# Attention beside a plain FFN: heads apart, and each weight piece converted over two steps

## The chip, the cores and the metric

The kernel runs on one core of one Trainium2 chip. The metric is the time of one execution on the device in microseconds, the median of the runs. The engines are called as the profile calls them: PE multiplies matrices (PEld loads its weights), DVE, ACT and POOL work on elements, and SP issues the transfers between HBM and the core's memory.

## The reference

Attention with a threshold over 8 batches and 8 heads (576 positions, head size 64), then one feed-forward layer with ELU over the 4608 tokens. The weights `w_in` (512 x 2048) and `w_out` (2048 x 512) arrive as 64-bit floats, everything else as 32-bit floats.

```python
scale = 1.0 / np.sqrt(q.shape[-1])
scores = scale * np.matmul(q, k.transpose(0, 1, 3, 2))
thresh = np.max(scores, axis=-1, keepdims=True) - tau
scores = np.where(scores >= thresh, scores, -1000000000.0)
scores = scores - np.max(scores, axis=-1, keepdims=True)
attn = np.exp(scores)
attn = attn / (np.sum(attn, axis=-1, keepdims=True) + 1e-09)
attn_out = np.matmul(attn, v)
x = attn_out.transpose(0, 2, 1, 3).reshape(B * S, H * D)
h = x @ w_in
g = np.where(h > 0.0, h, alpha * (np.exp(np.minimum(h, 0.0)) - 1.0))
out = g @ w_out
```

## The kernel before, in words

**Attention.** Two heads of a batch make a pair, and a pair is worked on in five *steps*: four of 128 query rows for both heads, and a fifth (i = 4) in which the last 64 rows of both heads fill one block of 128. In a step, PE makes the scores into PSUM (`scores`, tile `sc`); DVE takes each row's maximum (`mx`); from it come the bound of the mask (`th`, on POOL) and the bias of the exponential (`nb`); ACT makes the exponential `e`; DVE compares the scores with `th` and multiplies by `e` into `w`, with the row sum beside it (`masks`); DVE takes the reciprocal `rs`; POOL multiplies `w` by it (`normalize`). PE then turns `w` by blocks into the PSUM tiles `rt`, which ACT copies out (`turn_parts`, in two or three parts), and after two and five steps of a pair it multiplies by v (`values`, PSUM tile `pv`, copied out by ACT into `xt`). The tiles `pv` and `rt` share two PSUM buffers.

**Stages.** The first batch (20 steps) runs alone. The stage that the change touches is the next 15 steps, from `per_seq` to `SWITCH`; beside the attention of the second batch it runs the FFN of the first one in the plain way. Then come a stage of ten steps and the main stage, in which the FFN is done in another way with fewer products; the change leaves their work as it is, and only moves functions that the main stage defined to a place where both stages can use them.

**The FFN in this stage.** A unit of the first product (`ffn1`) is two halves of eight PE instructions each; when it is complete, ACT takes the exponential, POOL subtracts one (`minus`) and DVE makes the ELU by a minimum and a maximum (`elu`). A unit of the second product has two halves and no such work until its output is complete. `SHARES` says how many halves go into a step at each of three places: `after`, `second` and `carried`, whose work behind PE is left to the next step. `ffn_halves` takes a unit only when the weights that it needs are converted (`needs`). PE has two PSUM banks `f` for it.

**The weights.** A 64-bit float is loaded as two 32-bit words and made into a 32-bit float in pieces of 128 x 512, 32 in all. Each goes through a load into `wst` (four buffers, 512 KB), `convert_rest` (ACT, on the low words, in place), `convert_top` (DVE, two instructions into `wtop`, two buffers), `convert_add` (POOL), `convert_abs` (ACT, on the high words, in place) and `convert_end` (DVE, into the weight tiles). Six pieces are done in the first stage, and two in each step of this one. `load_w(4)` issues the next load if fewer than four pieces are loaded and not yet ended; the transfer has to wait until the piece that had the buffer before is ended.

**The order.** The stage is written under `manual_schedule`: each engine has one queue, and the instructions stand in it in the order in which the Python code emits them. In the kernel before, a step emits: loads of two pieces; scores; values; the first piece's top and add; the carried FFN work; the first turn; maxima of both heads in one instruction, `nb` and `th` on POOL, exponentials; the first piece's abs; FFN halves; the second piece's top, add and abs; the other turns and halves; masks; `minus`; both `convert_end`; `elu`; the normalize; the transposes and loads of the next pair (q in step i = 2, k in i = 3); and at last `convert_rest` of the two pieces of the next step. The scores of both heads lie in one PSUM tile of four banks, of which there is one.

Of the kernel before, what the change touches and what calls it, by code (L numbers as in the profile page):

```python
# [10 lines left out]
FP32 = mybir.dt.float32  # L11
U32 = mybir.dt.uint32
I32 = mybir.dt.int32
AF = mybir.ActivationFunctionType
# [5 lines left out]
def kernel(  # L20
# [90 lines left out]
    def load_w(ahead=2):  # L111
        i = progress[0]
        if i >= len(pieces) or i >= progress[1] + ahead:
            return
        progress[0] += 1
        src, dst, j, n = pieces[i]
        rows = src[j * P : (j + 1) * P]
        if src.dtype == FP32:
            nc.sync.dma_start(dst, rows[:, n : n + WN])
            return  # L120
        st = staged[i] = wstage.tile([P, WN, 2], U32, name="wst", bufs=4)
        nc.sync.dma_start(st.rearrange("p n w -> p (n w)"), rows.bitcast(U32)[:, 2 * n : 2 * (n + WN)])
# [8 lines left out]
    def convert_top(i):  # L131

        if i in staged:
            hi = staged[i][:, :, 1]
            top = tops[i] = wstage.tile([P, WN], U32, name="wtop", bufs=2)
            nc.vector.tensor_scalar(top, hi, 3, 0x3FFFFFFF, ALU.logical_shift_left, ALU.bitwise_and)
            nc.vector.scalar_tensor_tensor(top, hi, 0xC0000000, top, ALU.bitwise_and, ALU.bitwise_or)  # L137

    def convert_add(i):

        if i in staged:
            top = tops[i].bitcast(I32)
            nc.gpsimd.tensor_tensor(top, top, staged[i][:, :, 0].bitcast(I32), ALU.add)  # L143

    def convert_abs(i):
        if i in staged:
            mag = staged[i][:, :, 1].bitcast(FP32)
            nc.scalar.activation(mag, mag, AF.Abs)
# [95 lines left out]
    def exponentials(pr, i, hs):  # L244
        st = open_steps[pr, i]
        cs = slice(hs[0], hs[-1] + 1)
        src = st["both"] if len(hs) == 2 else st[hs[0]].unsqueeze(1)
        nc.vector.tensor_reduce(st["mx"][:, cs], src[:, :, :, :HALF], axis=AX.XY, op=ALU.max)  # L248
        nc.gpsimd.tensor_scalar(st["nb"][:, cs], st["mx"][:, cs], nkeep, 1.0, ALU.mult, ALU.mult)  # L249
        nc.gpsimd.tensor_scalar(st["th"][:, cs], st["mx"][:, cs], 1.0, ntau, ALU.mult, ALU.add)  # L250
        for h in hs:
            e = att.tile([P, 2, HALF], FP32, name="e")
            nc.scalar.activation(e, st[h][:, :, :HALF], AF.Exp, bias=st["nb"][:, h : h + 1], scale=keep)  # L253
            st[h] = st[h], e
# [15 lines left out]
    def normalize(pr, i, hs):  # L270
        st = open_steps[pr, i]
        for h in hs:
            wv = st["w"][:, h * S : (h + 1) * S]
            nc.gpsimd.tensor_scalar(wv, wv, st["rs"][:, h : h + 1], 1.0, ALU.mult, ALU.mult)  # L274

    def transpose(dst, src):
        nc.tensor.matmul(dst, src, ident, is_transpose=True, skip_group_check=True)  # L277
# [240 lines left out]
    def ffn_halves(n):  # L518
        after = []
        while n and (pending or units):  # L520
            if not pending:
                if needs(*units[0]) > progress[1]:
                    break
                f, a = units.popleft()
                parts, posts = f(*a)
                pending.extend((p, ()) for p in parts[:-1])
                pending.append((parts[-1], posts))
            p, posts = pending.popleft()
            p()
            after.append(posts)  # L530
            n -= 1
        return after

    def finish_units(after, engines):
        for posts in after:
            for post in posts[engines]:
                post()
# [38 lines left out]
        if hs == [1]:  # L576
            ahead(pr, i + 1)
    first.close()
    for name, bufs in (("s", 1), ("f", 2)):
        psum[name] = banks.enter_context(tc.tile_pool(name=f"ps_{name}", bufs=bufs, space=PSUM))  # L580

    while len(turned) > 1:
# [6 lines left out]
    SHARES = ((2, 1, 1), (1, 1, 0), (2, 1, 0), (1, 1, 0), (2, 1, 0))  # L589
    ACT, OTHER, ALL = slice(0, 1), slice(1, None), slice(0, None)  # L590
    with tc.manual_schedule():
        carried = []
        for _ in range(2):
            load_w(4)
        for n in range(per_seq, SWITCH):
            pr, i = step = steps[n]
            hs = heads_of(i)
            now = range(progress[1], min(progress[1] + 2, len(pieces)))
            if n == per_seq:
                for x in now:  # L600
                    convert_rest(x)
            for _ in now:
                load_w(4)
            scores(*step, hs)
            valued = steps[n - 2][1] in (1, NB - 1)
            if valued:
                out_values = values(steps[n - 2][0], 0 if steps[n - 2][1] == 1 else 1)
            parts = turn_parts(*steps[n - 1])
            for x in now[:1]:
                convert_top(x)  # L610
            finish_units(carried, slice(0, 2))
            for x in now[:1]:
                convert_add(x)
            copies = parts[0]()
            if not valued:
                copies()
            exponentials(*step, hs)
            finish_units(carried, slice(2, None))
            if valued:
                out_values()  # L620
                copies()
            for x in now[:1]:
                convert_abs(x)
            share = SHARES[n % NB]
            after = ffn_halves(share[0])
            finish_units(after, ACT)
            for x in now[1:]:
                convert_top(x)
                convert_add(x)
                convert_abs(x)  # L630
            parts[1]()()
            second = ffn_halves(share[1])
            finish_units(second, ACT)
            if len(parts) > 2:
                parts[2]()()
            carried = ffn_halves(share[2])
            masks(*step, hs)
            finish_units(after + second, slice(1, 2))
            for x in now:
                convert_end(x)  # L640
            finish_units(after + second, slice(2, None))
            normalize(*step, hs)
            if i in (2, 3):
                (prep_q if i == 2 else prep_k)(pr + 1)
                (copy_q if i == 2 else copy_k)(pr + 1)
            if i in (3, 4):
                load(pr + 2, ("qm",) if i == 3 else ("km",))
            if i == 3:
                load(pr + 1, ("v",))
            if steps[n - 2] == (NPAIR - 1, NB - 1):  # L650
                push_ffn(0)
            for x in range(progress[1], min(progress[1] + 2, progress[0])):
                convert_rest(x)
        finish_units(carried, ALL)
        turn(*steps[SWITCH - 1])
        finish_units(ffn_halves(len(pending)), ALL)
        behind(*steps[SWITCH - 2])
        behind(*steps[SWITCH - 1])
    assert progress[1] == len(pieces)
    assert units[0][1][0] == 1 and not pending  # L660
    banks.close()
    apart.append(True)
    for name, bufs in (("s", 2), ("f", 3), ("t", 1)):
        psum[name] = banks.enter_context(tc.tile_pool(name=f"ps_{name}2", bufs=bufs, space=PSUM))
    early.close()
# [80 lines left out]
    with tc.manual_schedule():  # L746
# [326 lines left out]
                    at(end + lag, f)  # L1073
                n -= 1

        def max_of(pr, i, h):
            st = open_steps[pr, i]
            nc.vector.tensor_reduce(st["mx"][:, h : h + 1], st[h][:, :, :HALF], axis=AX.XY, op=ALU.max)  # L1078

        def bound_of(pr, i, h):  # L1080
            st = open_steps[pr, i]
            nc.gpsimd.tensor_scalar(st["th"][:, h : h + 1], st["mx"][:, h : h + 1], 1.0, ntau, ALU.mult, ALU.add)  # L1082

        def exp_of(pr, i, h):
            st = open_steps[pr, i]
            nc.scalar.mul(st["nb"][:, h : h + 1], st["mx"][:, h : h + 1], nkeep)  # L1086
            e = att.tile([P, 2, HALF], FP32, name="e")
            nc.scalar.activation(e, st[h][:, :, :HALF], AF.Exp, bias=st["nb"][:, h : h + 1], scale=keep)  # L1088
            st[h] = st[h], e

        def mask_of(pr, i, h):
            st = open_steps[pr, i]
            if h == 0:
                st["w"] = wpool[0].tile([P, 2 * S], FP32, name="w")
            sc, e = st.pop(h)
            wv = st["w"][:, h * S : (h + 1) * S].rearrange("p (a n) -> p a n", a=2)
            nc.vector.scalar_tensor_tensor(wv, sc[:, :, :HALF], st["th"][:, h : h + 1], e, ALU.is_ge, ALU.mult,  # L1097
                                           accum_out=st["sm"][:, h : h + 1])

        def reciprocal_of(pr, i, hs):  # L1100
            st = open_steps[pr, i]
            cs = slice(hs[0], hs[-1] + 1)
            nc.vector.tensor_scalar(st["sm"][:, cs], st["sm"][:, cs], 1e-9, None, ALU.add)
            nc.vector.reciprocal(st["rs"][:, cs], st["sm"][:, cs])  # L1104

        begun = [0.0]

        def softmax(pr, i):
# [143 lines left out]
```

## Time and profile before

| | |
|---|---|
| time, median of three runs | 1388.53 us (1387.4 to 1390.45) |
| span of the profiled execution | 1384.1 us |
| matmuls (PE) busy in the span | 96% |
| DVE, POOL, ACT busy in the span | 77%, 60%, 46% |
| transfers | 259.82 MB, mean 188 GB/s |
| the stage of the change | about 105 to 239 us |

The busy share is an average over stages. PE's time is modelled and counts overlapping instructions once, so a high share doesn't mean that it runs at its peak. In the lists below a line of the timeline gives the start, the length, the engine, the line of the code, the operation, output and input with their shapes, how many instructions are merged, and in brackets how long the engine was idle before it and what ended that. SPq is the queue that issues transfers.

### The profile page before, as it was taken

The numbers are of one execution on the slowest core, as the hardware profiler recorded it, in microseconds if no ns is written. First come the engines' busy times: TensorE is split into PE (matmuls) and PEld (weight loads), VectorE is DVE, ScalarE is ACT, GpSimd is POOL, SyncE is SP. The second block draws the span as 40 slices with busy tenths as digits, with TensorE's granted clock in tenths as the row PEclk, the third lists the DMA queues.
The fourth block names the chain that finished last, engine by engine and source line by source line (L and its number), as shares of the span: only waits on it lengthen the run. The fifth ranks groups of instructions, "written<-read, shape, count | busy, mean of one in ns | idle before, by whom it ended". The sixth has DMA issues, their size and how long they took to land.

```text
span 1384.1 us, 21954 instructions
## 1 busy us (share of the span) xinstructions
PE 1334.5 (96%) x6566; PEld 988.6 (71%) x6566; DVE 1066.5 (77%) x2362; ACT 632.4 (46%) x1387; POOL 827.5 (60%) x1331
## 2 busy tenths in 40 slices
PE   6897989999999999999999999999999999999998
PEld 4554745747777777777777777777777777888886
DVE  6877885988888887888788978888888874545533
ACT  4666654325454445445453636263635452422421
POOL 5667773878657564756475747675666656414422
PEclk9999999999999999999999999999999999999999
DMA  5245451688897979898888988897889785411211
GB/s 114 58 91 148 132 148 44 187 244 254 226 261 221 280 214 255 209 266 240 230 231 256 251 222 236 236 258 212 239 230 275 217 241 146 133 58 64 92 57 31
DMA packets 316342, 259.82 MB, mean 188 GB/s; under 512 B 208320, under 2 KB 272320, under 8 KB 316224
## 3 DMA queue, kind: packets, MB, share of 16 engines
q1 hardware_dynamic: 316224, 258.42, 67.4%
q8 instruction: 53, 0.87, 0.3%
q14 instruction: 65, 0.53, 0.1%
HBM read 167.84 MB, written 90.51 MB: 187 GB/s over the span
## 4 chain that ended last, share of the span: by engine, by line
PE 76%; DVE 9%; ACT 5%; POOL 4%; issue 3%; DMA 1%; SPq 1%; DVEq 0%; POOLq 0%; ACTq 0%
PE f L999 28%; PE f L846 21%; PE sc L238 11%; PE pv L388 9%; PE pv L384 2%; PE f L435 2%; PE f L475 2%; ACT e L1088 2%; DVE w L265 2%; ACT e L253 1%; DVE mx L1078 1%; PE rt L277 1%; POOL wtop L143 1%; DVE mx L248 1%; DVE wtop L137 1%
## 5 line engine op out<-in xcount | busy, mean ns | idle before, releaser
L274 POOL TENSOR_SCALAR w<-w,rs 128x576 f32<-128x576 f32 x288 | 246.2, 860 | 108.4 <-DVE rs L1104 75.1
L1078 DVE TENSOR_REDUCE mx<-sc 128x1 f32<-128x576 f32 x207 | 148.0, 751 | 82.6 <-PE sc L238 82.6
L238 PE MATMUL sc<-kT,qT 64*128 64x288 f32 x1024 | 182.6, 440 | 22.1 <-DVE w L265 11.9
L348 DVE STREAM_TRANSPOSE x<-w 128x512 f32<-128x512 f32 (+1 forms) x350 | 182.5, 567 | 8.2 <-POOL w L274 8.2
L1086 ACT ACTIVATE nb<-mx,nkeep 128x1 f32<-128x1 f32 x207 | 61.4, 297 | 253.4 <-DVE mx L1078 253.4
L1088 ACT ACTIVATE e<-sc,nb,keep 128x576 f32<-128x576 f32 x207 | 172.1, 831 | 6.9
L1097 DVE SCALAR_TENSOR_TENSOR w<-sc,th,e 128x576 f32<-128x576 f32 x207 | 163.0, 810 | 8.6 <-ACT e L1088 0.4
L238 PEld LDWEIGHTS sc<-kT,qT 64*128 64x128 f32 x1024 | 100.7, 191 | 87.2 <-issue 51.8
L846 PE MATMUL f<-xt,sw 128*128 128x256 f32 x512 | 129.0, 389 | 1.0 <-DVE ot L1017 0.5
L846 PE MATMUL f<-xt,w_in_sb 128*128 128x256 f32 x512 | 125.1, 383 | 1.7 <-ACT w L860 1.5
L1082 POOL TENSOR_SCALAR th<-mx,ntau 128x1 f32<-128x1 f32 x207 | 54.3, 263 | 111.6 <-DVE mx L1078 111.4
L846 PEld LDWEIGHTS f<-xt,sw 128*128 128x128 f32 x512 | 93.2, 190 | 29.8 <-issue 13.5
L846 PE MATMUL f<-x,w_in_sb 128*128 128x256 f32 x448 | 109.0, 382 | 5.5 <-ACT g L913 5.5
L253 ACT ACTIVATE e<-sc,nb,keep 128x576 f32<-128x576 f32 x81 | 65.1, 830 | 104.2 <-POOL nb L249 103.2
L846 PEld LDWEIGHTS f<-xt,w_in_sb 128*128 128x128 f32 x512 | 95.7, 190 | 22.1 <-ACT xs L400 4.6
L999 PE MATMUL f<-w_out_sb,s 128*128 128x256 f32 x448 | 109.4, 387 | 0.0
L999 PE MATMUL f<-t,s 128*128 128x256 f32 x448 | 106.7, 381 | 0.6 <-POOL s L939 0.6
L999 PE MATMUL f<-w_out_sb,g 128*128 128x256 f32 x448 | 107.2, 382 | 0.0
L846 PEld LDWEIGHTS f<-x,w_in_sb 128*128 128x128 f32 x448 | 84.1, 190 | 21.2 <-ACT g L913 10.2
L999 PEld LDWEIGHTS f<-w_out_sb,s 128*128 128x128 f32 x448 | 82.3, 190 | 23.0 <-issue 13.2
L999 PEld LDWEIGHTS f<-w_out_sb,g 128*128 128x128 f32 x448 | 84.0, 190 | 15.8 <-ACT ge L879 3.5
L999 PEld LDWEIGHTS f<-t,s 128*128 128x128 f32 x448 | 84.0, 190 | 14.3 <-POOL s L939 3.4
(162 smaller groups left out, 2543.6 us busy)
## 6 DMA issues: line engine op xcount, KB each, us to landing
there<-x SPq DMA_DIRECT2D x500, 144.0 KB, 4.2
wTb<-there SPq DMA_DIRECT2D x75, 576.0 KB, 4.6
wTa<-there SPq DMA_DIRECT2D x50, 576.0 KB, 4.3
sw<-win_sums SPq DMA_DIRECT2D x62, 384.0 KB, 4.7
t<-wout_sums SPq DMA_DIRECT2D x45, 512.0 KB, 5.4
qm<-in_q_dram SPq DMA_DIRECT2D x128, 72.0 KB, 4.2
vm<-in_v_dram SPq DMA_DIRECT2D x64, 128.0 KB, 4.2
wst<-in_moe_w_in_dram SPq DMA_DIRECT2D x16, 512.0 KB, 4.5
```

The source lines that it names most:

```text
L238: nc.tensor.matmul(scs[h][:, a, :HALF], qs[r], kT[r, k0 : k0 + HALF], start=True, stop=True)
L253: nc.scalar.activation(e, st[h][:, :, :HALF], AF.Exp, bias=st["nb"][:, h : h + 1], scale=keep)
L274: nc.gpsimd.tensor_scalar(wv, wv, st["rs"][:, h : h + 1], 1.0, ALU.mult, ALU.mult)
L348: nc.vector.transpose(x[:, :, c0 : c0 + nc_], src.rearrange("p (c g n) -> p g c n", c=nc_, n=T))
L388: nc.tensor.matmul(pv[h * D : (h + 1) * D, g0 * T : g1 * T], vm[:, h, c], wT[:, g0:g1, h * (NC + 1) + c], start=False, stop=(c == NC - 1), ...
L846: nc.tensor.matmul(loc["banks"][place], left[:, j], right[:, j], start=(begins and j == 0), stop=(j == 1), skip_group_check=True)
L999: nc.tensor.matmul(place(m), lhs, rhs, start=(begins and v == 0), stop=(v == RU - 1), skip_group_check=True)
L1078: nc.vector.tensor_reduce(st["mx"][:, h : h + 1], st[h][:, :, :HALF], axis=AX.XY, op=ALU.max)
L1082: nc.gpsimd.tensor_scalar(st["th"][:, h : h + 1], st["mx"][:, h : h + 1], 1.0, ntau, ALU.mult, ALU.add)
L1086: nc.scalar.mul(st["nb"][:, h : h + 1], st["mx"][:, h : h + 1], nkeep)
L1088: nc.scalar.activation(e, st[h][:, :, :HALF], AF.Exp, bias=st["nb"][:, h : h + 1], scale=keep)
L1097: nc.vector.scalar_tensor_tensor(wv, sc[:, :, :HALF], st["th"][:, h : h + 1], e, ALU.is_ge, ALU.mult, accum_out=st["sm"][:, h : h + 1])
```

## The change

It changes one stage in three ways. The heads are taken apart: maximum, bound, bias and exponential are issued by head, the bias `nb` moves from POOL to ACT, and the scores lie in two PSUM tiles of two banks each in place of one of four. The conversion of a piece is spread over two steps: rest at the end of the step before, top and add in one step (`now`), abs and end in the next (`last`). And these pieces of work move: tops and adds go behind the masks and the normalize, one end goes between the maxima and the masks, the other behind the reciprocals, the loads go directly behind the ends, and an elu goes behind the add that follows its share. It is for keeping DVE from waiting for the exponential before the masks.

```diff
     first.close()
-    for name, bufs in (("s", 1), ("f", 2)):
+    apart.append(True)
+    for name, bufs in (("s", 2), ("f", 2)):
...
-        carried = []
+        carried, last = [], ()
...
-            now = range(progress[1], min(progress[1] + 2, len(pieces)))
+            now = range(progress[1] + len(last), min(progress[1] + len(last) + 2, len(pieces)))
             if n == per_seq:
                 for x in now:
                     convert_rest(x)
-            for _ in now:
-                load_w(4)
             scores(*step, hs)
...
             parts = turn_parts(*steps[n - 1])
-            for x in now[:1]:
-                convert_top(x)
             finish_units(carried, slice(0, 2))
-            for x in now[:1]:
-                convert_add(x)
+            for x in last[:1]:
+                convert_abs(x)
             copies = parts[0]()
             if not valued:
                 copies()
-            exponentials(*step, hs)
+            for h in hs:
+                max_of(pr, i, h)
+                bound_of(pr, i, h)
+                exp_of(pr, i, h)
             finish_units(carried, slice(2, None))
+            for x in last[1:]:
+                convert_abs(x)
+            for x in last[:1]:
+                convert_end(x)
+                load_w(4)
             if valued:
                 out_values()
                 copies()
-            for x in now[:1]:
-                convert_abs(x)
+            for h in hs:
+                mask_of(pr, i, h)
+            reciprocal_of(pr, i, hs)
+            for x in last[1:]:
+                convert_end(x)
+                load_w(4)
             share = SHARES[n % NB]
             after = ffn_halves(share[0])
             finish_units(after, ACT)
-            for x in now[1:]:
+            parts[1]()()
+            normalize(*step, hs)
+            for x in now[:1]:
                 convert_top(x)
                 convert_add(x)
-                convert_abs(x)
-            parts[1]()()
+            finish_units(after, slice(1, None))
             second = ffn_halves(share[1])
             finish_units(second, ACT)
             if len(parts) > 2:
                 parts[2]()()
+            for x in now[1:]:
+                convert_top(x)
+                convert_add(x)
+            last = now
             carried = ffn_halves(share[2])
-            masks(*step, hs)
-            finish_units(after + second, slice(1, 2))
-            for x in now:
-                convert_end(x)
-            finish_units(after + second, slice(2, None))
-            normalize(*step, hs)
+            finish_units(second, slice(1, None))
...
-            for x in range(progress[1], min(progress[1] + 2, progress[0])):
+            for x in range(progress[1] + len(last), min(progress[1] + len(last) + 2, progress[0])):
                 convert_rest(x)
...
     banks.close()
-    apart.append(True)
```

The functions `max_of`, `bound_of`, `exp_of`, `mask_of` and `reciprocal_of` are moved up from the main stage, unchanged.

More of the change, by code (lines that the diff above doesn't have):

```diff
@@ L274, in normalize, with max_of, bound_of, exp_of @@
             nc.gpsimd.tensor_scalar(wv, wv, st["rs"][:, h : h + 1], 1.0, ALU.mult, ALU.mult)
+    def max_of(pr, i, h):
+        st = open_steps[pr, i]
+        nc.vector.tensor_reduce(st["mx"][:, h : h + 1], st[h][:, :, :HALF], axis=AX.XY, op=ALU.max)
+    def bound_of(pr, i, h):
+        st = open_steps[pr, i]
+        nc.gpsimd.tensor_scalar(st["th"][:, h : h + 1], st["mx"][:, h : h + 1], 1.0, ntau, ALU.mult, ALU.add)
+    def exp_of(pr, i, h):
+        st = open_steps[pr, i]
+        nc.scalar.mul(st["nb"][:, h : h + 1], st["mx"][:, h : h + 1], nkeep)
+        e = att.tile([P, 2, HALF], FP32, name="e")
+        nc.scalar.activation(e, st[h][:, :, :HALF], AF.Exp, bias=st["nb"][:, h : h + 1], scale=keep)
+        st[h] = st[h], e
+    def mask_of(pr, i, h):
+        st = open_steps[pr, i]
+        if h == 0:
+            st["w"] = wpool[0].tile([P, 2 * S], FP32, name="w")
+        sc, e = st.pop(h)
+        wv = st["w"][:, h * S : (h + 1) * S].rearrange("p (a n) -> p a n", a=2)
+        nc.vector.scalar_tensor_tensor(wv, sc[:, :, :HALF], st["th"][:, h : h + 1], e, ALU.is_ge, ALU.mult,
+                                       accum_out=st["sm"][:, h : h + 1])
+    def reciprocal_of(pr, i, hs):
+        st = open_steps[pr, i]
+        cs = slice(hs[0], hs[-1] + 1)
+        nc.vector.tensor_scalar(st["sm"][:, cs], st["sm"][:, cs], 1e-9, None, ALU.add)
+        nc.vector.reciprocal(st["rs"][:, cs], st["sm"][:, cs])
     def transpose(dst, src):
@@ L1074, in ffn_quarters @@
                 n -= 1
[L1076 to L1104, printed above, removed]
         begun = [0.0]
```

## The prediction

> **What bounds the kernel now.** I read the page first (share of each engine), then busy time by stretch, then the DVE groups and the order of time in the stage that changes. The page:
>
> ```profile
> span 1384.1 us, 21954 instructions
> PE 1334.5 (96%) x6566; PEld 988.6 (71%) x6566; DVE 1066.5 (77%) x2362; ACT 632.4 (46%) x1387; POOL 827.5 (60%) x1331
> ```
>
> PE is nearly always busy over the whole span, so time is to be had or lost only where it is not. The changed stage runs from about 105 to 239 us. Busy time by stretch (columns: length, then PE, PEld, DVE, ACT, POOL busy, clock, DMA share, GB/s):
>
> ```profile
> 105.00:122.00 17.00, 11.23 (x58) 5.95 (x56) 12.74 (x24) 10.08 (x24) 10.51 (x12) 0.90 0.43 135
> 122.00:219.00 97.00, 86.74 (x423) 55.79 (x423) 83.94 (x153) 59.89 (x117) 72.20 (x79) 0.98 0.47 128
> 219.00:239.20 20.20, 19.41 (x96) 11.47 (x94) 7.23 (x16) 8.84 (x21) 5.79 (x13) 1.00 0.32 71
> ```
>
> In the 97 us in which weights are converted DVE is busy 87% and PE 89%, each waiting for the other; without conversions (the last row) PE alone sets the pace. The DVE waits from 105 to 217.5 us, and one step of DVE and POOL in order of time:
>
> ```profile
> DVE w L265 <- ACT e L253: 12.5, 13, 1.1
> ```
>
> ```profile
> 199.97 0.17 DVE L267 TENSOR_SCALAR sm<-sm 128x2 f32<-128x2 f32 x1
> 200.18 0.17 DVE L268 RECIPROCAL rs<-sm 128x2 f32<-128x2 f32 x1
> 200.26 1.27 DVE L155 SCALAR_TENSOR_TENSOR w_out_sb<-wst,wtop 128x512 f32<-128x512 f32 x2
> 200.52 2.43 POOL L274 TENSOR_SCALAR w<-w,rs 128x576 f32<-128x576 f32 x2 [1.72 <-DVE rs L268]
> 201.00 0.90 SPq L122 DMA_DIRECT2D wst<-in_moe_w_out_dram  x2
> 201.45 0.89 DVE L136 TENSOR_SCALAR wtop<-wst 128x512 uint32<-128x512 uint32 x1
> 202.38 1.11 DVE L137 SCALAR_TENSOR_TENSOR wtop<-wst,wtop 128x512 uint32<-128x512 uint32 x1
> 203.41 1.34 DVE L248 TENSOR_REDUCE mx<-sc 128x2 f32<-128x1152 f32 x1
> 203.72 1.29 POOL L143 TENSOR_TENSOR wtop<-wtop,wst 128x512 int32<-128x512 int32 x1 [0.77 <-DVE wtop L137]
> 204.99 0.44 POOL L249 TENSOR_SCALAR nb<-mx,nkeep 128x2 f32<-128x2 f32 x1
> 205.46 1.55 ACT L253 ACTIVATE e<-sc,nb,keep 128x576 f32<-128x576 f32 x2 [4.42 <-POOL nb L249]
> 207.13 0.82 DVE L265 SCALAR_TENSOR_TENSOR w<-sc,th,e 128x576 f32<-128x576 f32 x1 [1.10 <-ACT e L253]
> 210.84 1.27 ACT L129 ACTIVATE wst<-wst 128x512 int32<-128x512 uint32 x2
> ```
>
> Each two-head step loses about 1.1 us on DVE before its masks: the exponential waits for `nb`, which stands behind the weight add on POOL. That is what the change attacks. See also the buffers: the loads are issued at 201.0, at once when the old pieces have ended at 200.9 and 201.5, and ACT touches the new pieces (L129) only at 210.84. One more view, by the tile `wst`, gives the load:
>
> ```profile
> DMA to landing us min/median/max: 3.5/4.2/5.4
> ```
>
> So now a load has nearly a step (some 9 us) for its 4 us, and is never waited for.
>
> **What the Trainium skill says.** "PSUM — Partial Sum Buffer", Engine vs sequencer instructions: the ScalarE, VectorE and GpSimd queues are strictly first in, first out. The trace agrees: `nb` at 204.99 starts as the add that is ahead of it ends, although the maxima were ready at 204.75. "SBUF — State Buffer", two separate sides: DVE and GpSimd take a shared port pair as an exclusive lock. The trace agrees in kind: L136 takes 0.89 beside a normalize and 0.38 to 0.42 alone, L137 1.11 and 0.69. "DMA: Bandwidth & Descriptors", Rules for kernel authors: issue early, wait late. The trace before does so; the change does not, see below.
>
> **The change part by part.** I number the stage's steps 0 to 14, and call E the end of the second piece's `convert_end` in a step. In the trace before, E(1) is 122.2 and E(12) 219.0: 11 periods in 96.8 us, mean 8.8.
>
> *Heads apart.* One 1.34 us maximum becomes two (1.42 for both at 301.69), `nb` moves from POOL to ACT (0.3 us a head), the PSUM tile of four banks becomes two of two, so the next scores of a head need only that head's mask. About +0.1 us of DVE a step, and DVE no longer waits for POOL's add. The two `convert_end` are put around the masks, which fills the rest of the wait. By DVE work alone a step would be: the two `convert_top` (L136 and L137 each) 3.15 us (0.85+1.05 beside the normalize, 0.55+0.70 after it), maxima 1.35, first end 0.65, masks 1.57, sums and reciprocals 0.35, second end 0.65: 7.7 us, plus 0.6 for an elu and 0.7 for a q or k transpose. With 8.8 now, that would be the gain. The moved instructions on PE cost nothing: PE's order is the same before and after.
>
> *Two pieces kept over a step.* `wst` still has four buffers. Pieces of this step and of the last now hold all four, so a load cannot start before a `convert_end` in the middle of the step, and the second only at E. But `convert_rest` of both new pieces still stands on ACT at the end of the same step, ahead of the next step's `convert_abs`, copy, `nb` and exponentials. A load issued alone should land near the short end, 3.5 to 3.7 us (two at once took 4.2). From E: issue 0.07, landing and signal 3.75, rest 0.55, abs 0.57, copy of the turned block 0.5 gives 5.35; `nb` 0.33, exponential 0.73, `nb` 0.35, exponential 0.83 gives 7.6; second mask to the end of its sums 1.24, second end 0.68: next E at 9.5. In a step with values the copy is behind the exponentials: 9.0. With one head: 8.4. So a plain step is 9.5 where DVE needs 7.7: the wait removed is replaced by a longer one, for the load.
>
> *The elus.* In steps 2, 3, 4, 5 and 7 an FFN unit ends in the first share, and the order after E on DVE is then first `convert_top`, elu, second `convert_top`, next step's maxima. The elu needs POOL's `minus`, which stands in POOL's queue behind the normalize (to E+1.9) and the first `convert_add` (waits for L137, then 1.29: to E+3.3), and takes 0.62: the elu starts at E+3.95 where DVE was free at E+1.9, and the maxima, queued behind it, start at 5.7 (6.4 with a transpose). In the kernel before, `minus` is put ahead of the ends, so the elu waited only once from 105 to 217 us, for 1.3. Steps 4 and 6 have an elu behind the second add too, which starts the maxima at 8.4 and 5.9. From the start of the maxima to the next E it is 0.7 (maximum), 0.33 and 0.73 (`nb` and exponential), 0.35 and 0.83 (second head), 0.1, and 1.82 (second mask to E): 4.9, or 3.8 with one head.
>
> Each period with what ends last in it, in us after the E before:
>
> | to step | what ends last | us |
> |---|---|---|
> | 2 | load | 9.5 |
> | 3 | elu, transpose | 11.3 |
> | 4 | elu, transpose, one head | 10.2 |
> | 5 | two elus | 13.3 |
> | 6 | elu, and a carried elu after the maxima (its `minus` behind the second add: 8.4) | 11.6 |
> | 7 | late elu | 10.8 |
> | 8 | elu, transpose | 11.3 |
> | 9 | load, one head | 8.4 |
> | 10 | load | 9.6 |
> | 11 | load, values | 9.0 |
> | 12 | load | 9.5 |
>
> Sum 114.5, against 96.8: +17.7. *Ends of the stage.* Step 0 no longer ends pieces: from its maxima at 106.8, masks to 110.6, sums 0.4, tops 3.1 (with locks), maxima 1.4, end, masks, sums, end 3.3 more: E(1) at 118.8, 3.4 us ahead of before. At the other side step 13 now ends two pieces: its `xt` copy, for which PE's second turn waits, comes 7.7 us after E(12) = 233.3, and the scores of step 14 at 243.3, where before they began at 225.69. That is +17.6; PE sets the pace after that, as in the third stretch above, with the same work in the same order. PE's sum in steps 1 to 12 is about 88 us, so PE hides none of it. 1388.5 + 17.5 = **1406 us**.
>
> **Rivals.** (a) Only the load: the elus find their `minus` done (POOL's normalize and add being shorter when DVE idles speaks for it; the queue order against). Then the periods are 9.5, 9.3, 8.4, 9.6, 9.0, 9.5, 9.3, 8.4, 9.6, 9.0, 9.5: 101.1, E(12) at 219.9, step 14 about 4 us late: 1392.5. (b) Faster: the load lands before ACT asks and the elus are hidden, so DVE work is the bound: 7.7 a step plus elus and transposes, 6.3 with one head, about 89.5 in all, E(12) at 208.3, some 8 to 10 us ahead: 1380. For it speaks that 12.5 us of waits for the exponential go; against it that the four buffers leave no time for the load. (c) Slower still: loads at 4.5 or more (the trace has up to 5.4), with `th` pushed behind POOL's second add and locks (0.74 each beside DVE): +0.6 a step on 11 steps: 1413.
>
> **How the numbers follow.** Forecast 0.62, (a) 0.17, (b) 0.08, (c) 0.13. The range 1391 to 1414 takes in (a) and (c) and leaves out (b) and the tail. Faster 0.07, within 0.2% 0.04, slower 0.89.
>
> **What would show it.** Right: ACT idle before L129 until the DMA of `wst`, once in each of steps 1 to 11; DVE idle some 2 us before the elu until POOL's `minus`, in five steps; DVE waits for maxima or masks still there; PE waiting for the masks at the start of steps; the stage 17 us longer, nothing else changed. Wrong: `wst` landing before ACT gets to L129, or elus without a wait; then (b). If waits for the elu are under 1 us, (a).

## The result, and the profile after

| | before | after |
|---|---|---|
| time, median | 1389.49 us (1387.4 to 1391.05, 4 runs) | 1409.52 us (1408.24 to 1412.54, 4 runs) |
| ratio | | 1.0148, 95% interval 1.0126 to 1.017 |
| span, mean granted clock of the profile | 1384.1 us, 0.994 | 1406.4 us, 0.988 |

The change makes the kernel 20 us slower; forecast were 17.5. The first lines of the page after, and its busy time by stretch (columns as before), cut where its stage ends:

```profile
span 1406.4 us, 21971 instructions
PE 1345.0 (96%) x6566; PEld 993.9 (71%) x6566; DVE 1069.0 (76%) x2374; ACT 641.5 (46%) x1414; POOL 825.7 (59%) x1328
```

```profile
105.00:122.00 17.00, 12.89 (x65) 6.66 (x63) 12.04 (x24) 11.31 (x28) 8.57 (x11) 0.90 0.37 109
122.00:240.00 118.00, 97.22 (x441) 62.22 (x439) 86.12 (x164) 67.73 (x138) 71.69 (x79) 0.93 0.41 110
240.00:257.50 17.50, 14.93 (x66) 9.10 (x63) 8.60 (x18) 8.88 (x21) 7.34 (x12) 1.00 0.37 81
```

Only ACT has more to do, since it takes `nb` over from POOL. DVE's busy time is 1069.0 us against 1066.5, and PE is busy 10.5 us longer with the same 6566 instructions (the last section shows where most of that arises). In the stretch with conversions DVE is now busy 73% where it was 87%, and PE 82% where it was 89%. The work is spread over more time. The waits from 105 to 245 us say by what (columns: total us, times, longest):

```profile
DVE g L479 <- POOL g L475: 17.8, 8, 3.0
ACT wst L129 <- DMA wst<-in_moe_w_out_dram: 14.4, 8, 4.1
PE rt L307 <- ACT xt L425: 9.4, 2, 5.1
DVE w L297 <- ACT e L288: 6.3, 12, 1.4
ACT wst L129 <- DMA wst<-in_moe_w_in_dram: 4.4, 3, 2.7
```

The wait that the change attacks has gone down, from 16.0 us in 15 times to 6.3 in 12. Two have come in its place: 17.8 us of DVE in front of elus, and 14.4 + 4.4 us of ACT in front of freshly loaded weights. A third, PE's wait before a turn, which needs a PSUM buffer that the copy `xt` sets free, has grown from 3.5 us to 9.4.

The timeline of steps 1 to 3 shows both new waits at work:

```profile
117.22 1.28 POOL L143 TENSOR_TENSOR wtop<-wtop,wst 128x512 int32<-128x512 int32 x1
117.37 1.69 DVE L155 SCALAR_TENSOR_TENSOR w_in_sb<-wst,wtop 128x512 f32<-128x512 f32 x1
...
121.11 0.67 DVE L155 SCALAR_TENSOR_TENSOR w_in_sb<-wst,wtop 128x512 f32<-128x512 f32 x1
...
126.35 0.69 ACT L129 ACTIVATE wst<-wst 128x512 int32<-128x512 uint32 x1 [2.75 <-DMA wst<-in_moe_w_in_dram]
126.94 0.66 ACT L148 ACTIVATE wst<-wst 128x512 f32<-128x512 f32 x1
...
127.70 0.69 DVE L155 SCALAR_TENSOR_TENSOR w_in_sb<-wst,wtop 128x512 f32<-128x512 f32 x1 [1.78 <-ACT wst L148]
127.96 0.30 ACT L286 ACTIVATE nb<-mx,nkeep 128x1 f32<-128x1 f32 x1
...
129.23 0.82 DVE L297 SCALAR_TENSOR_TENSOR w<-sc,th,e 128x576 f32<-128x576 f32 x1 [0.84 <-ACT e L288]
...
131.69 2.44 POOL L274 TENSOR_SCALAR w<-w,rs 128x576 f32<-128x576 f32 x2 [4.20 <-DVE rs L304]
132.47 1.04 DVE L137 SCALAR_TENSOR_TENSOR wtop<-wst,wtop 128x512 uint32<-128x512 uint32 x1
134.09 1.29 POOL L143 TENSOR_TENSOR wtop<-wtop,wst 128x512 int32<-128x512 int32 x1
135.36 0.61 POOL L475 TENSOR_SCALAR g<-g 128x512 f32<-128x512 f32 x1
136.00 0.69 DVE L479 SCALAR_TENSOR_TENSOR g<-g,f 128x512 f32<-128x512 f32 x1 [2.50 <-POOL g L475]
```

Read it as two cycles. The load: the second end of step 1 stops at 121.78 and frees a buffer; the piece that goes into it reaches ACT at 126.35; `convert_rest` holds up the abs, `nb` and both exponentials behind it, and DVE waits for the abs (1.78) and for the exponential (0.84). The elu: normalize, add, `minus` stand in this order on POOL from 131.69 to 135.97, and DVE, done with its first top at 133.51, waits 2.50 us for the last of them.

### The profile page after: what moved, and what is told of

Same layout as the page of the kernel before. It is cut to its first block, busy times and chain, and to the rows that moved or that the text cites. A ratio compares the mean times of both kernels' runs of the same rounds, so it can differ in the third digit from the quotient of the medians.

```text
span 1406.4 us, 21971 instructions
## 1 busy us (share of the span) xinstructions
PE 1345.0 (96%) x6566; PEld 993.9 (71%) x6566; DVE 1069.0 (76%) x2374; ACT 641.5 (46%) x1414; POOL 825.7 (59%) x1328
## 4 chain that ended last, share of the span: by engine, by line
PE 69%; DVE 5%; ACT 4%; DMA 3%; POOL 3%; issue 2%; SPq 0%; DVEq 0%; ACTq 0%; POOLq 0%
PE f L1037 27%; PE f L884 20%; PE sc L238 9%; PE pv L418 7%; PE f L505 2%; DMA there<-x 2%; PE pv L414 2%; ACT e L288 2%; PE f L465 2%; DVE mx L278 1%; DVE w L297 1%; DMA wTa<-there 1%; DVE x L378 1%; ACT nb L286 1%; POOL w L274 1%
## 5 line engine op out<-in xcount | busy, mean ns | idle before, releaser
L278 DVE TENSOR_REDUCE mx<-sc 128x1 f32<-128x576 f32 x234 | 167.1, 750 | 87.9 <-PE sc L238 87.8
L238 PE MATMUL sc<-kT,qT 64*128 64x288 f32 x1024 | 185.8, 440 | 19.6 <-DVE kT L200 8.3
L297 DVE SCALAR_TENSOR_TENSOR w<-sc,th,e 128x576 f32<-128x576 f32 x234 | 184.8, 811 | 19.2 <-ACT e L288 8.1
L288 ACT ACTIVATE e<-sc,nb,keep 128x576 f32<-128x576 f32 x234 | 194.5, 831 | 7.8
L286 ACT ACTIVATE nb<-mx,nkeep 128x1 f32<-128x1 f32 x234 | 69.2, 296 | 265.7 <-DVE mx L278 265.7
L238 PEld LDWEIGHTS sc<-kT,qT 64*128 64x128 f32 x1024 | 102.1, 191 | 86.7 <-issue 51.0
L282 POOL TENSOR_SCALAR th<-mx,ntau 128x1 f32<-128x1 f32 x234 | 64.1, 276 | 120.5 <-DVE mx L278 119.6
L884 PEld LDWEIGHTS f<-xt,sw 128*128 128x128 f32 x512 | 93.2, 190 | 29.8 <-issue 13.5
L884 PEld LDWEIGHTS f<-x,w_in_sb 128*128 128x128 f32 x448 | 84.1, 190 | 21.2 <-ACT g L951 10.2
L903 POOL TENSOR_TENSOR u<-u,w 128x256 f32<-128x256 f32 x64 | 49.1, 768 | 69.2 <-ACT u L898 65.7
```

The costliest lines, as they stand in the source:

```text
L238: nc.tensor.matmul(scs[h][:, a, :HALF], qs[r], kT[r, k0 : k0 + HALF], start=True, stop=True)
L884: nc.tensor.matmul(loc["banks"][place], left[:, j], right[:, j], start=(begins and j == 0), stop=(j == 1), skip_group_check=True)
L903: nc.gpsimd.tensor_tensor(loc[name], x(), loc[other], op)
```

## Experiments

Times are compared with runs of the kernel before on the same chip: 1388.61 us (1385.73 to 1390.47, 10 runs) for the two waits and for the heads apart alone, 1390.18 (1387.72 to 1392.06, 7) for the six buffers, the two other orders and the heads joined, and 1390.29 (1386.96 to 1392.81, 8) for the two kernels without adds. A ratio is to those runs, so a difference of medians from two such groups can be some us off it.

**The two waits, each taken away alone and together.** The first kernel puts `convert_rest` ahead of its own top, so that it no longer stands at the end of a step:

```diff
             for x in now[:1]:
+                convert_rest(x)
                 convert_top(x)
...
-            for x in range(progress[1] + len(last), min(progress[1] + len(last) + 2, progress[0])):
-                convert_rest(x)
```

(with the same line ahead of the second top, and without the loop that did it for the first step).

> The changed kernel with convert_rest of a piece moved from the end of the step before to directly ahead of its own convert_top, so that ACT does not stand before a load that has just been issued; the elus stay behind the adds. Theory (two waits, load and elu): ACT's 19 us of waits for the DMA go, but in the steps with an elu the elu's wait ends last and stays (17.8 us on DVE); only the periods to steps 2 and 9 to 12 shorten, by 1.5 to 2 us each: 1409.5 falls to about 1400. Rival (the load alone is the cause, the elus are beside it): about 1385. Rival (the elus alone): no change, 1409.

Measured: 1405.34 us (1403.06 to 1409.93), 1.0127 (1.0102 to 1.0152). The second puts `minus` ahead of the normalize and of the second top:

```diff
+            finish_units(after, slice(1, 2))
             normalize(*step, hs)
...
-            finish_units(after, slice(1, None))
+            finish_units(after, slice(2, None))
             second = ffn_halves(share[1])
...
+            finish_units(second, slice(1, 2))
             for x in now[1:]:
...
-            finish_units(second, slice(1, None))
+            finish_units(second, slice(2, None))
```

> The changed kernel with POOL's minus of a unit moved ahead of the normalize (first share) and ahead of the second convert_add (second share); convert_rest stays at the end of the step. Theory (two waits): DVE's 17.8 us of waits for minus go nearly all, the load's wait then ends last in every step, periods 8.4 to 9.8: about 1396, still slower than the kernel before. Rival (elus alone): about 1385. Rival (load alone): no change, 1409.

Measured: 1405.72 us (1401.21 to 1406.96), 1.0119 (1.0096 to 1.0143). The third has both edits.

> Both moves together. Theory: neither wait is left, DVE work bounds a step at 7.7 us plus elus and transposes, about 1380 to 1386, faster than the kernel before (1389.5). Rival (PE's wait for the copy of xt, which stands behind the exponentials in steps with values, takes their place): about 1390.

Measured: 1394.87 us (1392.54 to 1398.87, 6 runs), 1.0046 (1.0029 to 1.0064). All three fall less than the theory said, and of the third's two forecasts the rival's time (1390) is nearer. The waits went as meant. With the rests late no wait for the DMA of `wst` is left, and the elus' is as it was:

```profile
DVE g L479 <- POOL g L475: 17.9, 8, 3.0
```

With `minus` early it is the other way round:

```profile
ACT wst L129 <- DMA wst<-in_moe_w_out_dram: 13.4, 7, 3.5
ACT wst L129 <- DMA wst<-in_moe_w_in_dram: 5.6, 4, 3.3
DVE g L479 <- POOL g L475: 2.5, 2, 1.8
```

The periods from the second end of one step to that of the next, read off the DVE timelines of the profiled runs (us), tell where the time is:

| to step | 2 | 3 | 4 | 5 | 6 | 7 | 8 | 9 | 10 | 11 | 12 | sum |
|---|---|---|---|---|---|---|---|---|---|---|---|---|
| before | 8.8 | 9.5 | 8.0 | 9.1 | 8.9 | 10.2 | 9.1 | 7.4 | 8.3 | 8.8 | 8.8 | 96.8 |
| after | 10.3 | 11.2 | 10.1 | 12.7 | 11.5 | 11.4 | 11.2 | 8.7 | 9.8 | 9.7 | 9.5 | 116.0 |
| rests late | 8.5 | 11.2 | 10.1 | 12.8 | 11.6 | 11.4 | 11.2 | 9.0 | 8.6 | 8.5 | 8.5 | 111.1 |
| `minus` early | 10.3 | 9.5 | 9.6 | 11.9 | 9.8 | 10.5 | 9.5 | 8.7 | 10.3 | 9.3 | 9.4 | 108.9 |
| both | 8.5 | 9.5 | 9.6 | 9.9 | 9.9 | 10.5 | 9.5 | 8.3 | 8.5 | 8.5 | 8.5 | 101.3 |

Taking the load's wait away helps steps 2 and 10 to 12 and no other; taking the elus' away helps steps 3 to 8. That is the division that the prediction's table made, but for step 9, which it gave to the load. (The periods of `minus` early are those of its fastest run, 1401.21 us, so they show more of a gain than its median.) In step 5 each hides behind the other: 12.8 and 11.9 alone, 9.9 together. And with hardly anything left of either, a plain step (two heads, no elu, no transpose) still takes 8.5 us, where the prediction had 7.7 for DVE's work.

**Where the buffers come in.** Six buffers of `wst` in place of four, all else as in the change:

```diff
-        st = staged[i] = wstage.tile([P, WN, 2], U32, name="wst", bufs=4)
+        st = staged[i] = wstage.tile([P, WN, 2], U32, name="wst", bufs=6)
...
-                load_w(4)
+                load_w(6)
```

(and four loads in place of two where the stage begins).

> The changed kernel with six buffers wst in place of four and loads up to six pieces ahead; convert_rest stays at the end of the step. Theory (the load is late because the pieces in flight hold all four buffers): ACT's waits for the DMA go as they did with convert_rest moved, and the time is the same as there, 1403 to 1407. Rival (the place of convert_rest ahead of the exponentials costs by itself, with or without a load to wait for): it stays at 1409.

Measured: 1405.81 us (1403.33 to 1409.89), 1.0117 (1.0091 to 1.0143): as expected, and the same as rests late. No wait for the DMA is left, so the load was late because all four buffers were held, not because the transfer is slow.

**What is left of the loss.** With both waits gone, DVE is busy longer than before. From the second end of step 1 to that of step 12, first with both edits, then before the change:

```profile
122.20:223.50 101.30, 91.39 (x427) 58.72 (x423) 92.04 (x162) 67.80 (x140) 72.59 (x77) 0.95 0.51 129
```

```profile
122.20:219.00 96.80, 86.74 (x423) 55.79 (x423) 83.74 (x153) 59.69 (x117) 72.00 (x79) 0.98 0.47 128
```

DVE is busy 92.0 us in place of 83.7, for the same work; it has nine more instructions, since the maximum of two heads has become two. Groups of DVE from 122 to 222 us (count, busy us, mean ns), with both edits and then before:

```profile
L137 DVE SCALAR_TENSOR_TENSOR wtop<-wst,wtop 128x512 uint32<-128x512 uint32 x22 | 25.2, 1148 | 0.8
L155 DVE SCALAR_TENSOR_TENSOR w_out_sb<-wst,wtop 128x512 f32<-128x512 f32 x13 | 11.6, 894 | 0.0
L136 DVE TENSOR_SCALAR wtop<-wst 128x512 uint32<-128x512 uint32 x22 | 9.9, 452 | 0.0
```

```profile
L137 DVE SCALAR_TENSOR_TENSOR wtop<-wst,wtop 128x512 uint32<-128x512 uint32 x22 | 17.7, 803 | 0.8
L155 DVE SCALAR_TENSOR_TENSOR w_out_sb<-wst,wtop 128x512 f32<-128x512 f32 x16 | 10.2, 678 | 0.0
L136 DVE TENSOR_SCALAR wtop<-wst 128x512 uint32<-128x512 uint32 x22 | 14.2, 647 | 0.0
```

The second instruction of the top (L137) and the ends (L155) take longer; the top's first instruction (L136) takes less and gives about half of L137's part back. Two places of the timeline with both edits, a second top of step 2 and the ends of a plain step, show what stands beside them:

```profile
133.09 1.67 DVE L137 SCALAR_TENSOR_TENSOR wtop<-wst,wtop 128x512 uint32<-128x512 uint32 x1
...
208.76 2.97 POOL L143 TENSOR_TENSOR wtop<-wtop,wst 128x512 int32<-128x512 int32 x2
209.25 1.41 DVE L278 TENSOR_REDUCE mx<-sc 128x1 f32<-128x576 f32 x2
210.58 1.70 DVE L155 SCALAR_TENSOR_TENSOR w_out_sb<-wst,wtop 128x512 f32<-128x512 f32 x1
...
214.33 0.67 DVE L155 SCALAR_TENSOR_TENSOR w_out_sb<-wst,wtop 128x512 f32<-128x512 f32 x1
```

The first end starts in the second add on POOL, is held until that ends at 211.73, and then takes its usual 0.55 to 0.6. The second end, with no add beside it, takes 0.67. The top at 133.09 stands beside the first add (132.70 to 134.20) in the same way. The Trainium skill's "SBUF — State Buffer", two separate sides, says that the shared port pair is an exclusive lock, which an operation of VectorE with two inputs in SBUF takes against one of GpSimd that reads SBUF; the end is such an operation, and 1.70 us against 0.67 agrees.

Three kernels on this. The first moves the first end behind the reciprocals, away from the add:

```diff
-            for x in last[:1]:
-                convert_end(x)
-                load_w(4)
...
             reciprocal_of(pr, i, hs)
-            for x in last[1:]:
+            for x in last:
```

> The kernel with both moves, and the first convert_end put behind the masks and reciprocals beside the second. In the kernel with both moves DVE is 91% busy and L155 takes 0.87 us in the mean in place of 0.71, since the first end meets POOL's second add. Theory (the change also makes DVE's two-input operations meet POOL's work, and the lock costs DVE time): L155 falls back to about 0.7, one of some 1.0 us saved in the plain steps, 1389 to 1392 after 1395. Rival (the saved time comes back as a wait of the masks for the exponential, which the end had filled, or the lock moves on to another operation): 1394 to 1397.

Measured: 1409.92 us (1404.9 to 1413.53), 1.014 (1.0114 to 1.0167). That is above both ranges. The end does fall to a mean of 0.79 us for `w_in` and 0.71 for `w_out` (0.87 and 0.89 with both edits), but, as the rival had it in kind, `convert_top`'s first instruction, L136, rises from 0.45 to 0.82, and the wait before the masks is back:

```profile
ACT wst L148 <- DVE wtop L137: 11.1, 7, 2.2
DVE w L297 <- ACT e L288: 9.9, 18, 1.4
```

So the place between maxima and masks is worth having: the end stands there in time in which DVE would otherwise wait for the exponential.

The second goes after PE's wait instead, and copies `xt` and the turned block ahead of the maxima in steps with values:

```diff
             copies = parts[0]()
-            if not valued:
-                copies()
+            if valued:
+                out_values()
+            copies()
...
-            if valued:
-                out_values()
-                copies()
```

> The kernel with both moves, and in steps with values the copies of xt and of the turned block ahead of the exponentials on ACT. Theory (DVE's work with its locks bounds this kernel): PE's 9.3 us of waits for xt shrink, the time stays within 1393 to 1397. Rival (PE's wait for xt is what is left of the loss): 1386 to 1390.

Measured: 1401.78 us (1398.79 to 1402.77), 1.0081 (1.0064 to 1.0097), slower than with both edits alone (1394.87) and above both ranges. PE's wait for `xt` is gone, but DVE waits 9.0 us for exponentials (4.6 with both edits), and PE 5.9 us for second-product weights (0.3). This order doesn't win back what is left of the loss.

The third leaves the adds out, once with both edits and once in the kernel with the heads apart alone (its edit is below), as a control. In both, `convert_add(x)` is taken out of the stage's two loops, and the low words are missing from 24 pieces of weights.

> Both waits removed (rests ahead of their tops, minus and elu ahead of the adds), and in addition the two adds of a step on POOL are left out in the changed stage: the low words are missing from those 24 pieces of weights, so the work of 24 instructions of 1.29 us on POOL is not done. Theory (what is left of the loss is DVE held up by POOL's adds through the shared port): the weight operations on DVE fall to L155 0.68 and L137 0.75 us or less in the mean, and the time falls from 1395 to 1380 to 1387. Rival (the extra step of lag and the order on ACT and PE keep the time): L155 and L137 fall as well, but the time stays at 1391 to 1396.

> The control to the run before it: heads apart alone, with the conversion in one step as before, and the same adds on POOL left out in this stage. Theory (the adds cost little here, since they seldom meet the weight operations): 1375 to 1379, so the two kernels without adds lie at most 8 us apart where with adds they lie 15 apart. Rival: the adds cost as much here (a fall of 8 us or more), so that the distance between the two kernels stays at 12 to 17 us and the locks with the adds don't explain it.

Measured: with both edits 1385.29 us (1381.88 to 1387.37), 0.9957 (0.9937 to 0.9976); the control 1379.21 us (1378.5 to 1380.19), 0.9921 (0.9904 to 0.9938). Without adds the first falls by 10 us and the control by 1 (by the ratios 12 and 4); the distance between the two conversions shrinks from 15 us (1394.87 to 1379.97) to 6 (by the ratios from 13.5 to 5). DVE in the stage without adds, from the second end of step 1 to that of step 12:

```profile
121.93:212.66 90.73, 85.68 (x428) 55.86 (x430) 84.29 (x162) 67.98 (x139) 42.04 (x55) 1.00 0.56 143
```

The same top as above, and the first end of a plain step:

```profile
132.34 0.69 DVE L137 SCALAR_TENSOR_TENSOR wtop<-wst,wtop 128x512 uint32<-128x512 uint32 x1
...
208.78 0.68 DVE L155 SCALAR_TENSOR_TENSOR w_out_sb<-wst,wtop 128x512 f32<-128x512 f32 x1
```

So the adds are what made these two long: 1.67 falls to 0.69, and 1.70 to 0.68. The same 162 instructions of DVE take 84.3 us where they took 92.0, and plain steps take 7.7 to 8.2 us in place of 8.5. The adds in their new place cost about 9 of the 15 us (8.5 of 13.5 by the ratios; the intervals of the four kernels leave some 5 us of doubt on it). That they cost time here and little in the control is shown. That the lock alone does it isn't: without adds the end also no longer has an add to wait for, and POOL has `th` sooner. L137 is one place where the expectation was off: its mean fell to 0.98 only, not 0.75; beside the normalize it still takes 1.03. No run tries to take the last 6 us away, but the traces of the two kernels without adds place most of them: from the second end of step 1 to that of step 12 they take 90.7 us and 88.3 (heads alone), and from there to the scores of step 14 9.6 and 6.6, since with the conversion in two steps step 13 still has two pieces to end.

**The parts of the change.** Heads apart alone, in the kernel before:

```diff
-    for name, bufs in (("s", 1), ("f", 2)):
+    apart.append(True)
+    for name, bufs in (("s", 2), ("f", 2)):
...
-            exponentials(*step, hs)
+            for h in hs:
+                max_of(pr, i, h)
+                bound_of(pr, i, h)
+                exp_of(pr, i, h)
```

> The kernel before with the heads taken apart and nothing else: two PSUM tiles for the scores, maximum, bound, bias (on ACT) and exponential by head, in the order of before; pieces are converted within one step as before. Theory: the wait of 1.1 us before the masks goes without a new one: some 10 us faster than before, about 1378 to 1383. Rival (heads apart brings nothing, because the second maximum and the bound behind POOL's add cost as much): 1388 to 1391.

Measured: 1379.97 us (1377.99 to 1383.38, 5 runs), 0.9949 (0.9932 to 0.9967): faster than the kernel before, by 8.6 us (7 by the ratio, whose interval is 4.6 to 9.4 us), and the best of all kernels with the whole computation. DVE's wait before the masks is gone but for this (16.0 us in 15 times before):

```profile
DVE w L265 <- ACT e L288: 2.9, 5, 1.4
```

And the change without it, the heads joined as before and the conversion in two steps:

> The change without heads apart: one PSUM tile of four banks, one maximum for both heads, nb on POOL, as before; the conversion over two steps and all its moves as in the change. Theory (heads apart is the good part, the two-step conversion the bad one): slower than the changed kernel, whose second add on POOL now stands ahead of nb: 1413 to 1422. Rival (the parts need each other, heads apart costs here): below 1409.

The edit is the reverse: `exponentials(*step, hs)` in place of the calls by head, one `s` tile, `apart.append(True)` back behind `banks.close()`. Measured: 1426.25 us (1424.7 to 1427.43), 1.026 (1.0244 to 1.0275), slower than expected (1413 to 1422). So the heads apart are worth 8.6 us by themselves and about 16 within the change (1.026 against 1.0148), and the conversion in two steps with its new order costs about 29 us on top of them (+20.0 against -8.6).

## Why the prediction was right

*Heads apart* was right: the wait for the exponential went down, and alone it gives 8.6 us, with DVE's work about as before.

*Two pieces kept over a step* was right in mechanism and within 0.8 us a step. The landing was taken as 3.7; the tile `wst` from 105 to 245 us shows

```profile
DMA to landing us min/median/max: 3.3/3.7/5.0
```

ACT waits for the DMA in eleven places, 18.8 us; a twelfth, 3.0 us at 135.98 in step 2, is put down to `minus`, which ended in that same moment. Steps 2, 10 and 11 came out longer (10.3, 9.8, 9.7 against 9.5, 9.6, 9.0): in step 1 the rest started 4.6 us after the end that freed its buffer, not 3.8. A slip stands in the sum as well: the five terms from E to the copy add to 5.44, not 5.35, which would make the plain period 9.6.

*The elus* were right: eight waits, 2.2 us in the mean, in the steps named. Step 5 was put 0.6 too high and step 7 as much too low, and it is luck that the two cancel. The sum of periods is 116.0 against 114.5.

*Ends of the stage* is the step that was off. E(1) was put at 118.8, 3.4 us ahead of before, and is 121.78: 0.4 ahead. Three terms: the first maxima start at 108.09 in place of 106.8; from there to the end of the masks step 0 takes 4.65 us in place of 3.8, and its `nb` starts at 109.68 behind the copies of a turn on ACT, though the maximum that it needs was there at about 108.9; and the first end of step 1 takes 1.69 and not 0.65, beside an add. From there the working holds: E(12) is 237.76 against 233.3, and the scores of step 14 begin at 248.00 against 243.3. That is +22.3 from before, against +17.6: 3.0 of the difference comes from E(1), 1.5 from the periods, 0.2 from what follows. The two profiled executions as a whole differ by the same 22.3 us (1384.1 and 1406.4), so the later stages give nothing back; the medians differ by less, 20.0, since the profiled execution before (1385.93 us) lay further below its median than the one after.

*Rival (b)* was lost by more than its argument. It took 7.7 us for DVE's work in a plain step. With both waits removed a plain step takes 8.5, and the term that was mis-sized is the first end: 0.65 alone, 1.70 beside the add on POOL. (The tops, put at 3.15, take 2.8; the masks wait 0.2 for `th`.) Over the eleven steps the rival put 89.5 us; with both edits they take 101.3, and without the adds too 90.7. So even with both waits removed this order was not faster than before (1394.87).

## What to carry to other kernels

Before you spread a conversion over more steps, count its buffers: with four held by pieces under way the next load can't start early, and an instruction that needs it, standing early in a queue that works in order, holds up everything behind it. When a filler goes into the gap of another engine's wait, see what runs beside it on the port that they share; a 0.67 us operation took 1.70. And try the parts of a change one by one: here one part was worth 8.6 us and the other lost 29.

## What the runs showed of the hardware

In this stage a long wait of PE cost more than its length. Matmuls of PE after two waits, and the same groups without one:

```profile
126.65 0.60 PE L307 MATMUL rt<-ident,w 128*128 128x128 f32 x4
...
135.32 1.89 PE L465 MATMUL f<-xt,w_in_sb 128*128 128x256 f32 x8
142.28 1.09 PE L307 MATMUL rt<-ident,w 128*128 128x128 f32 x4 [5.07 <-ACT xt L425]
143.16 3.62 PE L465 MATMUL f<-xt,w_in_sb 128*128 128x256 f32 x8
...
175.89 1.09 PE L307 MATMUL rt<-ident,w 128*128 128x128 f32 x4 [3.16 <-issue]
176.77 3.62 PE L465 MATMUL f<-xt,w_in_sb 128*128 128x256 f32 x8
```

Twelve matmuls take 4.7 us where they take 2.5. The granted clock is 0.50 from 142.28 to 146.60 us and from 175.89 to 180.20, and 0.93 in the mean from 122 to 240 us. PE is busy 95.2 us from E(1) to E(12) for work that took 86.7. The Trainium skill's "TensorE: Matmul & The Clock Gate", Part 1: The HAM clock gate, says that an idle window of about 3.4 us puts the array at half rate until it has been busy about as long. The trace agrees for the waits of 4.32 and 5.07 us. Near that figure it gives no sharp limit: a wait of 3.16 us, which is shorter, was followed by half rate too, and after one of 3.22 us, at 227.56, the clock was 1.00 and the groups took their usual 0.63 and 1.88. How much of it reaches the end was not tried; from E(1) to E(12) DVE waited for scores once, for 0.65 us.
